# The last output tile of an attention and gated-FFN kernel in column blocks of 256, 128, 64 and 64

## The chip, the cores and the metric

The kernel runs on one core of a Trainium2 chip. In the profiles PE is TensorE, which does the matmuls, ACT is ScalarE, DVE is VectorE and SP is SyncE; a trailing q marks the engine's instruction queue, which waits and issues transfers while the engine itself counts as idle. L385 is line 385 of that run's kernel. The metric is the device time of one execution in microseconds. The profile gives one execution as a trace; its span runs from the first to the last instruction and is some 1.8 us shorter than the time.

One quantity of this document: the **tail**, from the start of the first matmul of the last output tile to the end of the span, read from a trace. "At 2.45 us" means 2.45 us after that first matmul. A store "lands" when the profile shows it finished. Positions in the tail, landings and ends are read from the packed traces in nanoseconds and rounded to 0.01 us, so a difference of two rounded times can be off by 0.01. The expectations were written from spans rounded to 0.1 us and so differ by up to 0.04: tails of 5.75 for 5.78, 6.00 and 5.96 for 6.01 and 5.99, 6.48 for 6.44; 2.53, 2.38 and 2.86 for the 2.55, 2.40 and 2.82 from the last issue to the end.

## The reference, cut to what matters

```
x: 8 batches, 8 heads, 512 rows, 64      state: 8, 8, 32, 64
xread = softmax(x state^T / 8) state     sread = softmax(state x^T / 8) x
y   = concat(xread, sread) as rows of 512            # 8 * (512 + 32) = 4352 rows
out = (relu(y w_gate) * (y w_val)) w_out             # d_ff = 1536, fp32 out
```

The output is written in tiles of 128 rows by 512 columns. Each tile is a sum over 12 slices of d_ff, that is 12 matmuls with 128x128 weights.

## The kernel before: the parts that matter

Matmul results lie in one of eight PSUM banks; output tiles alternate between two of them, 6 and 7. A copy by ScalarE or VectorE takes a result to one of four staging buffers, and a store takes it from there to memory.

```python
opool = pool("opool", 4)                              # four staging buffers "o_sb"
given, turn = [], {"r": 0, "o": 1}

def bank(name, kind="r"):
    if given:
        n = given.pop(0)                              # a bank named by hand
    ...
    else:
        n = turn["r"] % 6 if kind == "r" else 6 + turn["o"] % 2
        turn[kind] += 1
    return psum.tile([128, 512], FP32, name=name, tag=f"b{n}")

def fin_x(b, tsub, eng="act"):                        # an ordinary output tile
    o_sb = opool.tile([128, d_model], FP32, name="o_sb", tag="o_sb")
    copy[eng](out=o_sb, in_=held["o", b, tsub])
    n = 2 if b == B - 2 or (b == B - 1 and tsub == 0) else 1
    for i in range(n):                                # stored whole or in two halves of rows
        rows = slice(128 // n * i, 128 // n * (i + 1))
        nc.sync.dma_start(out=out_rows(b, tsub)[rows], in_=o_sb[rows])

def out_last(b, tsub):                                # the last tile, in column blocks
    for lo, n, eng, q in ((0, 256, nc.scalar.copy, nc.scalar), (256, 128, nc.scalar.copy, nc.scalar),
                          (384, 128, nc.vector.tensor_copy, nc.sync)):
        cols = slice(lo, lo + n)
        ps = o_bank()[:, 0:n]                         # bank("o_ps", "o"): 6 and 7 in turn
        for jf in range(NF):
            nc.tensor.matmul(ps, hsb[b][:, jf, ...], wo_sb[:, jf, cols], ...)
        o_sb = opool.tile([128, d_model], FP32, name="o_sb", tag="o_sb")
        eng(out=o_sb[:, 0:n], in_=ps)
        q.dma_start(out=out_rows(b, tsub)[:, cols], in_=o_sb[:, 0:n])
```

The softmax here doesn't subtract the row's maximum and nothing guards it: scores larger than these inputs give would overflow.

Of the kernel before, what the change touches and what calls it, by code (L numbers as in the profile page):

```python
# [16 lines left out]
def kernel(  # L17
# [9 lines left out]
    nc = tc.nc  # L27

    B, H, S, D = x.shape
# [316 lines left out]
    def o_bank():  # L346
        return bank("o_ps", "o")
# [8 lines left out]
    def out_rows(b, tsub):  # L356
        return out[b * SP: b * SP + S].rearrange("(p q) m -> q p m", q=NC)[tsub]

    def fin_x(b, tsub, eng="act"):
        o_sb = opool.tile([128, d_model], FP32, name="o_sb", tag="o_sb")  # L360
        copy[eng](out=o_sb, in_=held["o", b, tsub])  # L361
        n = 2 if b == B - 2 or (b == B - 1 and tsub == 0) else 1
        for i in range(n):
            rows = slice(128 // n * i, 128 // n * (i + 1))
            nc.sync.dma_start(out=out_rows(b, tsub)[rows], in_=o_sb[rows])
# [9 lines left out]
    def out_last(b, tsub):  # L375

        for lo, n, eng, q in ((0, 256, nc.scalar.copy, nc.scalar), (256, 128, nc.scalar.copy, nc.scalar),
                              (384, 128, nc.vector.tensor_copy, nc.sync)):
            cols = slice(lo, lo + n)
            ps = o_bank()[:, 0:n]  # L380
            for jf in range(NF):
                nc.tensor.matmul(ps, hsb[b][:, jf, tsub * 128:(tsub + 1) * 128], wo_sb[:, jf, cols],  # L382
                                 start=(jf == 0), stop=(jf == NF - 1))
# [3 lines that stand above are left out]
# [5 lines left out]
    def out_piece(b, i):  # L392
        out_part(b, i)
        if i % 3 == 2:
            fin_x(b, i // 3)
# [37 lines left out]
    def spin(n, cols=512):  # L433
        for i in range(n):
# [6 lines left out]
             "sc": att_sc, "ex": att_exp, "nr": att_sum, "nx": att_scale, "aT2": att_T2, "ao2": att_out2, "aT": att_T, "ao": att_out,  # L441
             "c": c_unit, "co": c_out, "u": u_unit, "uo": u_out, "gv": gv, "re": relu, "mu": mult, "o": out_part,
             "of": fin_x, "xn": x_next, "xp": x_pad, "sr": sr_mm, "sn": sr_norm}
    program = """
    dx.1.0.2 dx.1.1.2 stc.0.0.act stc.0.1.act xc.0.0.dve dw.0.0.128 spin.7 stT.0@4 xc.0.1.act dw.1.0.128 on xT.0.0@2
# [86 lines left out]
    for g in range(first, NF * (B + 1)):  # L532
        b, jf = divmod(g, NF)
# [14 lines left out]
    for i in range(NF - lag % NF, NF - 3):  # L548
        out_piece(B - 1, i)
    out_last(B - 1, NC - 1)  # L550


# [28 lines left out]
```

## Time and profile before

| | before |
|---|---|
| median time (6 runs, 222.99 to 223.83) | 223.5 us |
| span of the profiled run | 221.7 us |
| PE busy | 97% of the span |
| first matmul of the last tile | 215.95 us |
| issue of the last store | 219.17 us, so at 3.23 us |
| from that issue to the end of the span | 2.55 us |
| tail | 5.78 us |

The lines that show the tail are quoted in the prediction. This is the view of waits for SyncE in the last microseconds of the kernel before (engine and line, what it waited for: us in total, times, longest):

```profile
SPq L386 <- DVE o_sb L385: 2.0, 1, 2.0
SPq L365 <- ACT o_sb L361: 1.7, 1, 1.7
SPq L576 <- DMA out_dram<-o_sb: 0.8, 2, 0.4
SPq L576 <- PEq L576: 0.7, 2, 0.5
```

Line 576 is the end of the program. Two of its waits for stores took 0.4 us each, the rest found their store already landed.

### The profile page before, as it was taken

The numbers are of one execution on the slowest core, as the hardware profiler recorded it, in microseconds if no ns is written. First come the engines' busy times: TensorE is split into PE (matmuls) and PEld (weight loads), VectorE is DVE, ScalarE is ACT, GpSimd is POOL, SyncE is SP. The second block draws the span as 40 slices with busy tenths as digits, with TensorE's granted clock in tenths as the row PEclk, the third lists the DMA queues.
The fourth block names the chain that finished last, engine by engine and source line by source line (L and its number), as shares of the span: only waits on it lengthen the run. The fifth ranks groups of instructions, "written<-read, shape, count | busy, mean of one in ns | idle before, by whom it ended". The sixth has DMA issues, their size and how long they took to land.

```text
span 221.7 us, 4851 instructions
## 1 busy us (share of the span) xinstructions
PE 216.0 (97%) x1959; PEld 106.3 (48%) x1959; DVE 130.5 (59%) x228; ACT 124.8 (56%) x238; POOL 49.4 (22%) x54
## 2 busy tenths in 40 slices
PE   7799999999999999999999999999999999999994
PEld 3454455444554444444444444445444445666544
DVE  2697898965786569664767378646874433222100
ACT  5489888565767555564466456645654444222222
POOL 8777826460004233015000700000000000000000
PEclk9999999999999999999999999999999999999999
DMA  6999999182065962771169114501311112222332
GB/s 156 174 195 197 203 237 276 43 154 86 4 146 188 146 233 79 156 240 51 50 146 278 53 47 101 104 34 50 95 50 47 49 47 50 50 47 55 89 95 95
DMA packets 37879, 25.48 MB, mean 115 GB/s; under 512 B 18944, under 2 KB 33280, under 8 KB 37856
## 3 DMA queue, kind: packets, MB, share of 16 engines
q1 hardware_dynamic: 24992, 16.85, 28.7%
q0 software_dynamic: 11968, 7.47, 21.7%
q10 hardware_dynamic: 896, 0.85, 1.4%
q8 instruction: 15, 0.25, 0.5%
q14 instruction: 8, 0.07, 0.1%
HBM read 18.35 MB, written 8.91 MB: 123 GB/s over the span
## 4 chain that ended last, share of the span: by engine, by line
PE 85%; DMA 12%; POOL 1%; issue 0%; DVE 0%; POOLq 0%; DVEq 0%
PE o_ps L353 39%; PE gv_ps L316 32%; DMA xb<-in_x_dram 9%; PE gv_ps L333 5%; PE up L291 4%; DMA wg_sb<-in_moe_w_gate_dram 4%; PE sr_ps L264 1%; PE sc_ps L200 1%; PE o_ps L382 1%; PE xT_ps L186 0%; POOL xb L415 0%; PE stT_ps L129 0%; PE aT_ps L235 0%; PE srT_ps L277 0%; PE upc L291 0%
## 5 line engine op out<-in xcount | busy, mean ns | idle before, releaser
L353 PE MATMUL o_ps<-wo_sb,h_sb 128*128 128x512 bf16 x372 | 94.8, 379 | 0.0
L316 PE MATMUL gv_ps<-ans,U 128*128 128x512 bf16 x384 | 94.4, 379 | 0.0
L344 DVE TENSOR_TENSOR h_sb<-gv_ps,g_sb 128x512 bf16<-128x512 f32 x96 | 65.0, 689 | 43.5 <-ACT g_sb L340 42.1
L340 ACT ACTIVATE g_sb<-gv_ps 128x512 bf16<-128x512 f32 (+1 forms) x108 | 62.9, 588 | 45.9 <-PE gv_ps L316 35.0
L316 PEld LDWEIGHTS <-U 128*128 128x128 bf16 x384 | 36.1, 98 | 40.7 <-issue 0.4
L353 PEld LDWEIGHTS <-h_sb 128*128 128x128 bf16 x372 | 35.3, 98 | 39.7 <-issue 1.6
L361 ACT COPY o_sb<-o_ps 128x512 f32<-128x512 f32 x31 | 18.3, 590 | 17.4 <-PE o_ps L353 17.4
L301 ACT CAST U<-up 128x512 bf16<-128x512 f32 x36 | 18.9, 593 | 12.1 <-PE up L291 12.0
L142 POOL CAST xb<-xf 128x1024 bf16<-128x1024 f32 x10 | 10.6, 1088 | 66.4 <-DMA xf<-in_x_dram 45.4
L301 DVE CAST U<-up 128x512 bf16<-128x512 f32 x36 | 22.7, 684 | 4.1 <-PE up L291 3.7
L256 POOL COPY xa<-xb 128x2048 bf16<-128x2048 bf16 (+1 forms) x9 | 15.5, 1748 | 0.3
L213 DVE TENSOR_REDUCE cs<-e_sn 128x16 f32<-128x512 bf16 x16 | 10.9, 683 | 7.3 <-ACT e_sn L207 7.3
L344 DVE TENSOR_TENSOR hs_sb<-gv_ps,g_sb 128x256 bf16<-128x256 f32 x12 | 5.1, 425 | 15.3 <-PE gv_ps L333 10.8
L207 ACT ACTIVATE e_sn<-sc_ps 128x512 bf16<-128x512 f32 x16 | 9.6, 600 | 7.4 <-PE sc_ps L200 7.4
L219 DVE TENSOR_TENSOR a_sn<-e_sn,rc 128x512 bf16<-128x512 bf16 x16 | 12.4, 778 | 0.4
L291 PEld LDWEIGHTS <-stT 64*32 64x32 bf16 x512 | 5.9, 90 | 9.5 <-issue 8.1
L311 ACT CAST U<-upc 128x512 bf16<-128x512 f32 (+1 forms) x21 | 10.1, 570 | 0.5 <-PE upc L291 0.4
L200 PEld LDWEIGHTS <-xT 128*128 128x128 bf16 x128 | 5.7, 98 | 4.1 <-DVE xT L177 0.8
L291 PE MATMUL up<-wg_sb,stT 64*32 64x512 bf16 x144 | 7.5, 382 | 0.0
L291 PE MATMUL up<-wv_sb,stT 64*32 64x512 bf16 x144 | 7.2, 380 | 0.0
L333 PE MATMUL gv_ps<-br,wg_sb 128*128 128x256 bf16 x48 | 7.2, 273 | 0.0
L333 PE MATMUL gv_ps<-br,wv_sb 128*128 128x256 bf16 x48 | 7.2, 273 | 0.0
(63 smaller groups left out, 121.5 us busy)
## 6 DMA issues: line engine op xcount, KB each, us to landing
out_dram<-o_sb SPq DMA_DIRECT2D x26, 256.0 KB, 2.4
xf<-in_x_dram SPq DMA_DIRECT2D x4, 1024.0 KB, 6.3
wo_sb<-in_moe_w_out_dram POOLq DMA_DIRECT2D x2, 768.0 KB, 14.5
wg_sb<-in_moe_w_gate_dram POOLq DMA_DIRECT2D x5, 256.0 KB, 8.6
wv_sb<-in_moe_w_val_dram POOLq DMA_DIRECT2D x5, 256.0 KB, 10.5
out_dram<-o_sb SPq DMA_DIRECT2D x10, 128.0 KB, 2.4
xf<-in_x_dram POOLq DMA_DIRECT2D x1, 1024.0 KB, 16.1
xb<-in_x_dram POOLq DMA_DIRECT2D x3, 256.0 KB, 6.8
```

The lines of the kernel that those rows point to most:

```text
L142: copy[eng](out=xb[b][:, :, hs].rearrange("p c h d -> p h c d"), in_=xf[b][:, hs])
L213: nc.vector.reduce_sum(out=cs, in_=e_v, axis=AX.X)
L219: {"dve": nc.vector, "pool": nc.gpsimd}[eng].tensor_tensor(out=by_pair(a_sn[b], jp).rearrange("p r (j n) -> p r j n", n=Ns), in0=e_v, in1= ...
L256: nc.gpsimd.tensor_copy(out=v[:, hs:hs + src.shape[1]], in_=src)
L291: nc.tensor.matmul(dst[parity][32 * j:32 * j + 32], stT[r:r + 64, b, j, 32 * parity:32 * parity + 32], wsb[r:r + 64, j, lo:lo + n], start= ...
L301: copy[eng](out=U[b][:, w, kc, lo:lo + 512], in_=held["u", b, w, lo][kc])
L316: nc.tensor.matmul(ps[w], U[b][:, w, kc, f0:f0 + 128], ANS[b][:, kc].rearrange("p c t -> p (c t)"), start=(kc == 0), stop=(kc == NK - 1))
L333: nc.tensor.matmul(ps[w][:, 0:nt], wsb[:, j, f0:f0 + 128], br[:, j].rearrange("p b n -> p (b n)"), start=(j == 0), stop=(j == NJ - 1))
L340: nc.scalar.activation(out=g_sb[:, 0:n], in_=ps[0][:, 0:n], func=AF.Relu)
L344: nc.vector.tensor_tensor(out=dst, in0=ps[1][:, 0:n], in1=held["g", b, jf][:, 0:n], op=ALU.mult)
L353: nc.tensor.matmul(held["o", b, tsub], src[:, jf, tsub * 128:(tsub + 1) * 128], wo_sb[:, jf], start=(jf == 0), stop=(jf == NF - 1))
L361: copy[eng](out=o_sb, in_=held["o", b, tsub])
```

## The change

Its intent: the path after the last matmul is a copy, a store and the close. A last block of 64 columns in place of 128 makes that copy and that store smaller, while the rest of the columns are copied and stored beside the matmuls. One other store, 12 us ahead, becomes one transfer in place of two halves.

```diff
-        n = 2 if b == B - 2 or (b == B - 1 and tsub == 0) else 1
+        n = 2 if b == B - 2 else 1
...
-                              (384, 128, nc.vector.tensor_copy, nc.sync)):
+                              (384, 64, nc.vector.tensor_copy, nc.sync), (448, 64, nc.vector.tensor_copy, nc.sync)):
```

## The prediction

> **What bounds the kernel now.** I read the page first: PE is busy 97% of the span, so until about 218.8 us of a span of 221.7 us the matmuls set the time. The diff touches only the last tile, so I went to the end of the span. The chain of waits there (start us, us, what):
>
> ```profile
> by line: PE o_ps L353 55.9%; PE o_ps L382 15.7%; PE gv_ps L333 9.6%; DVE o_sb L385 1.7%; issue 0.3%; DVEq L385 0.2%
> ...
> 207.48 8.63 PE o_ps L353 x40
> 216.11 2.67 PE o_ps L382 x36
> 218.78 0.04 DVEq L385
> 218.81 0.04 issue
> 218.85 0.29 DVE o_sb L385
> ```
>
> The reader is to see that the 36 matmuls of the last tile (line 382: three blocks of 12) run without a gap behind the tile before, and that after them only one VectorE copy remains, then its store. The timeline shows who does what in that tail:
>
> ```profile
> 215.95 2.81 PE L382 MATMUL o_ps<-wo_sb,h_sb 128*128 128x256 bf16 x36
> 216.15 0.59 ACT L361 COPY o_sb<-o_ps 128x512 f32<-128x512 f32 x1 [2.00 <-PE o_ps L353]
> 216.76 0.35 SPq L365 DMA_DIRECT2D out_dram<-o_sb  x1
> 217.46 0.37 ACT L385 COPY o_sb<-o_ps 128x256 f32<-128x256 f32 x1 [0.72 <-PE o_ps L382]
> 217.86 0.36 ACTq L386 DMA_DIRECT2D out_dram<-o_sb  x1
> 218.39 0.27 ACT L385 COPY o_sb<-o_ps 128x128 f32<-128x128 f32 x1 [0.56 <-PE o_ps L382]
> 218.69 0.36 ACTq L386 DMA_DIRECT2D out_dram<-o_sb  x1
> 218.85 0.29 DVE L385 COPY o_sb<-o_ps 128x128 f32<-128x128 f32 x1 [10.84 <-PE o_ps L382]
> 219.17 0.35 SPq L386 DMA_DIRECT2D out_dram<-o_sb  x1
> ```
>
> Matmuls end at 215.95 + 2.81 = 218.76; VectorE starts 0.09 later, copies until 219.14; the store is issued at 219.17. The DMA view gives that store 1.6 us to landing, so 220.8; closing semaphores fill the last 0.9 us. After 218.76 only this one path matters: copy, issue, landing, close, 2.9 us in all. The change means to shorten the copy and the store on it.
>
> The 36 matmuls also fix the blocks in time. A burst of matmuls of 128 columns and one of 64 columns, both with 128x128 weights, stand elsewhere in the timeline:
>
> ```profile
> 45.56 0.39 PE L235 MATMUL aT_ps<-id,a_sn 128*128 128x128 bf16 x4
> 57.25 0.40 PE L200 MATMUL sc_ps<-stT,xT 128*128 128x64 bf16 x8
> ```
>
> One of 128 columns lasts 0.219 us and one of 64 lasts 0.193 us (groups by form). So the pitch is (0.39 - 0.219)/3 = 0.057 us at 128 columns and (0.40 - 0.193)/7 = 0.030 us at 64: half the columns cost half the time, and the weight load doesn't hold a 64-column stream. Counted back from 218.76, the last matmul starts at 218.54, the third block at 218.54 - 11 x 0.056 = 217.93, and the second ends at about 218.09.
>
> **What the Trainium skill says.** "TensorE: Matmul & The Clock Gate", section "Back-to-back issue gap", gives about 60 cycles (25 ns) for up to 64 columns and 134 for 128. The trace agrees within 5 ns (30 and 57 ns). "PSUM — Partial Sum Buffer", section "PSUM bank collisions raise a hardware error", says that a matmul writing and another engine reading the same bank must be kept apart by a semaphore, by bank and not by address. The trace before shows no PE wait in the tail, but this decides the case after the change. "VectorE: DVE Perf Modes", in the errata section, gives a PSUM read 120 cycles plus one per fp32 element: 258 ns at 128 elements, where the trace has 292; the page's fixed part is too small here, its slope fits. "DMA: Bandwidth & Descriptors", section "Specifications", says that runs under 512 B are read-modify-written; no store in the tail before has such runs (a row of 128 fp32 is just 512 B), so the trace can't confirm it for stores.
>
> **The change part by part.**
>
> First part: the store of tile 0 of the last batch becomes one DMA of 256 KB instead of two halves, near 203.8 us. It saves SyncE one issue of about 0.47 us (median of that line), while SyncE has nothing to do until about 209. Its buffer is taken again only at 216.15, some 12 us later. Worth 0.
>
> Second part: the last 128 columns become 64 + 64.
> - Matmuls: 12 x 0.056 = 0.67 us become 24 x 0.030 = 0.71 us: +0.04 if nothing waits.
> - Copy: the cast of 512 fp32 from PSUM takes 684 ns on VectorE and the copy of 128 takes 292, a slope of (684 - 292)/384 = 1.02 ns per element. At 64: 292 - 65 = 227 ns, so -0.065 on the path. The copy of the third block lies beside the matmuls of the fourth.
> - Store: 64 columns are 32 KB instead of 64, but still 128 rows. The store's data moves in about 0.4 us of its 1.6; I give it 0 to -0.1 from the smaller rows, with the read-modify-write as the opposite risk.
> - SyncE: with no wait the third block's copy would end near 218.77 and its issue run from 218.80 to 219.15, so the fourth's issue would start at 219.15: no gain against 219.17.
>
> So even undisturbed this is worth 0 to 0.1 us.
>
> **The new wait.** The output banks are two and alternate. Before, the tile before used one, block 1 the other, block 2 the first again, block 3 the one of block 1, freed at 217.46 + 0.37 = 217.83, just ahead of its use at 217.93. The fourth block needs the bank of block 2, which ScalarE reads from 218.39 to 218.66. (It starts that late, though the matmuls ended at 218.09, since ScalarE was issuing block 1's store until 218.22.) The third block's matmuls now start their last at 217.93 + 11 x 0.030 = 218.26; the fourth could start at 218.29, but must wait until 218.66 plus a semaphore. The wait of the first score matmuls for VectorE shows about 0.06 us from the end of the copy (5.54 + 0.82 = 6.36) to the matmul (6.42). So: first matmul 218.72; last 218.72 + 11 x 0.030 = 219.05; its end + 0.193 = 219.24; VectorE + 0.09 = 219.33; + 0.227 = 219.56; issue + 0.03 = 219.59. Against 219.17 that is **+0.42 us**. If the weight load is also held, add up to 0.1; for the smaller store take off up to 0.1. Sum: +0.4 us, 223.5 + 0.4 = 223.9 us.
>
> **The rivals.**
> - No bank wait in effect (ScalarE would read block 2 sooner, or the wait be shorter): 223.4 to 223.5. Against it: ScalarE's work before that copy isn't changed, so 218.66 should stand.
> - The staging buffers become the wait. There are four, and the fourth block takes the one of tile 2, whose store is issued at 216.76. At 2.0 us to landing (DMA view of the tail) it is free at 218.8, half a microsecond before the copy at 219.33. Hidden; if it landed 1 us late, it would add 0.5: 224.4.
> - The 256-byte rows cost more to write: if the store takes twice its data time, +0.4: 224.3. The trace has only reads of that size.
> - ScalarE or SyncE becomes the bound: SyncE's two issues are 0.35 each and, with the bank wait, 0.8 apart, so no.
>
> **Range and chances.** All of these move tenths of a microsecond. Three runs before spread from 222.99 to 223.83, so the noise is as large as the effect. From 223.2 (no wait, a low draw) to 224.5 (wait plus slow small rows). A change over 2% would need 4.5 us, more than the whole tail of 2.9 us after the last matmul. So within 2% is 0.98 likely; of the rest slower takes a little more.
>
> **What would show it.** In the changed trace: the pitch of line 382 near 0.030 us in the 64-column blocks; a gap of about 0.4 us in its matmuls, ended by ScalarE's copy of block 2; VectorE copies near 227 ns; the last SyncE issue about 0.4 us later; the single store of tile 0 without effect. I'd be wrong if the matmuls ran on without a gap, if the last copy waited for a DMA, or if the last store's landing differed clearly from 1.6 us.

## The result, and the profile after

The changed kernel takes 223.84 us median (six runs, 223.24 to 224.29) against 223.5; the ratio is 1.0016 with an interval of 0.9995 to 1.0037. Within 2%, as forecast, and 0.06 us from the forecast time.

The timeline of the tail of the changed kernel (start us, us, engine, line, what; in brackets the idle time ahead of it and what ended it):

```profile
216.50 2.49 PE L382 MATMUL o_ps<-wo_sb,h_sb 128*128 128x256 bf16 x36
218.42 0.36 ACTq L386 DMA_DIRECT2D out_dram<-o_sb  x1
218.95 0.27 ACT L385 COPY o_sb<-o_ps 128x128 f32<-128x128 f32 x1 [0.56 <-PE o_ps L382]
219.09 0.22 DVE L385 COPY o_sb<-o_ps 128x64 f32<-128x64 f32 x1 [10.52 <-PE o_ps L382]
219.26 0.51 PE L382 MATMUL o_ps<-wo_sb,h_sb 128*128 128x64 bf16 x12 [0.27 <-ACT o_sb L385]
219.34 1.11 SPq L386 DMA_DIRECT2D out_dram<-o_sb  x2
219.87 0.22 DVE L385 COPY o_sb<-o_ps 128x64 f32<-128x64 f32 x1 [0.55 <-PE o_ps L382]
```

The matmuls no longer run through. The first three blocks end at 216.50 + 2.49 = 218.99; then PE stands idle for 0.27 us until 219.26, and what ended that is ScalarE's copy, which ends at 218.95 + 0.27 = 219.22. The chain of what ended last says the same, step by step (start us, us, what):

```profile
218.01 0.38 ACT o_sb L385
218.40 0.02 issue
218.42 0.36 ACTq L386
...
218.95 0.28 ACT o_sb L385
219.22 0.04 issue
219.26 0.53 PE o_ps L382 x12
219.79 0.03 DVEq L385
219.82 0.04 issue
219.87 0.22 DVE o_sb L385
```

Before, this chain went straight down PE. Now it runs over ScalarE: copy of block 1, issue of block 1's store, copy of block 2, and only then the fourth block's matmuls.

The last store is issued at 220.12, which is 3.61 us after the first matmul at 216.50: 0.39 later than before. But the span ends only 6.01 us after that matmul, a tail 0.23 us longer. So 0.15 us came back after the last issue: 2.40 us from there to the end against 2.55.

### The profile page after: what moved, and what is told of

Read it like the earlier page. It is cut to its first block, busy times and chain, and to the rows that moved or that the text cites. A ratio compares the mean times of both kernels' runs of the same rounds, so it can differ in the third digit from the quotient of the medians.

```text
span 222.5 us, 4849 instructions
## 1 busy us (share of the span) xinstructions
PE 213.6 (96%) x1942; PEld 106.6 (48%) x1971; DVE 130.5 (59%) x229; ACT 124.7 (56%) x238; POOL 48.9 (22%) x54
## 4 chain that ended last, share of the span: by engine, by line
PE 93%; DMA 3%; issue 2%; ACT 0%; POOL 0%; ACTq 0%; DVE 0%; POOLq 0%; DVEq 0%
PE o_ps L353 38%; PE gv_ps L316 37%; PE gv_ps L333 5%; PE up L291 4%; DMA xb<-in_x_dram 3%; PE sc_ps L200 2%; PE upc L291 2%; PE sr_ps L264 1%; PE xT_ps L186 1%; PE o_ps L382 1%; PE warm_ps L435 1%; PE aT_ps L235 1%; PE xT_ps L173 0%; PE stT_ps L129 0%; ACT o_sb L385 0%
## 5 line engine op out<-in xcount | busy, mean ns | idle before, releaser
L316 PE MATMUL gv_ps<-ans,U 128*128 128x512 bf16 x372 | 93.1, 379 | 0.6 <-issue 0.2
L353 PE MATMUL o_ps<-wo_sb,h_sb 128*128 128x512 bf16 x358 | 91.8, 379 | 2.0 <-issue 1.7
L142 POOL CAST xb<-xf 128x1024 bf16<-128x1024 f32 x10 | 10.1, 1040 | 66.8 <-DMA xf<-in_x_dram 61.9
```

Of the source, the lines that this page charges most:

```text
L316: nc.tensor.matmul(ps[w], U[b][:, w, kc, f0:f0 + 128], ANS[b][:, kc].rearrange("p c t -> p (c t)"), start=(kc == 0), stop=(kc == NK - 1))
L353: nc.tensor.matmul(held["o", b, tsub], src[:, jf, tsub * 128:(tsub + 1) * 128], wo_sb[:, jf], start=(jf == 0), stop=(jf == NF - 1))
```

## The experiments

All tails in one table. "Lands after" is counted from the last store's issue. "Waits behind" counts SyncE's closing waits for other transfers that still follow the last store's own. "Close" is the time from the last store's issue to the end of the span. Ratios are to the kernel before, from five rounds; the changed kernel's is from the six runs of each.

| run | last store issued at | lands after | waits behind | close | tail | ratio (95%) |
|---|---|---|---|---|---|---|
| before | 3.23 | 1.63 | 0 | 2.55 | 5.78 | |
| changed | 3.61 | 1.47 | 0 | 2.40 | 6.01 | 1.0016 (0.9995 to 1.0037) |
| after_again | 3.62 | 1.47 | 0 | 2.38 | 5.99 | 1.0027 (1.0006 to 1.0048) |
| four_banks | 3.28 | 1.55 | 0 | 2.47 | 5.75 | 1.0013 (0.9993 to 1.0034) |
| store0_sync | 3.35 | 1.46 | 0 | 2.38 | 5.73 | 1.0017 (0.9999 to 1.0036) |
| three_blocks | 3.16 | 1.69 | 0 | 2.62 | 5.77 | 1.0001 (0.9983 to 1.0020) |
| store_only | 3.22 | 1.62 | 1 | 2.61 | 5.84 | |
| split_only | 3.62 | 1.47 | 7 | 2.82 | 6.44 | |
| same_bank | 3.72 | 1.47 | 0 | 2.39 | 6.11 | |
| last_128 | 3.95 | 1.61 | 0 | 2.54 | 6.48 | |
| four_banks_stage | 3.28 | 1.54 | 0 | 2.47 | 5.75 | 0.9986 (0.9965 to 1.0008) |
| free_store0_sync | 3.26 | 1.53 | 0 | 2.44 | 5.70 | 1.0003 (0.9971 to 1.0034) |
| one_more_store | 3.23 | 1.63 | 7 | 2.96 | 6.19 | 1.0002 (0.9972 to 1.0031) |
| merge_elsewhere | 3.62 | 1.46 | 0 | 2.39 | 6.01 | 0.9978 (0.9952 to 1.0003) |

The close is the landing plus a remainder. Where no wait stands behind the last store's, the remainder is 0.91 to 0.93 us in all eleven profiles.

How to weigh the two kinds of number: all the tails differ by at most 0.8 us, while the first matmul of the last tile started anywhere from 215.25 to 216.71 us in these profiles, with the same program in front of it but for single stores. That scatter of the 215 us ahead lies on every time and is larger than the effect, so the times can't rank these kernels. Part of it is the granted TensorE clock: every timed run whose mean clock was 0.991 or 0.992 took 223.77 us or more (median 224.27), while the median of the others was 223.28. In the profiles of that kind (the changed kernel's is one) the clock is 0.91 in the first 20 us, where the kernel before has 1.00. Steps inside the tail repeat to 0.01 us (3.61 and 3.62; ScalarE's store of block 2 at 2.74 in nearly all), so they can. Each tail is that of a single profile; three profiles with the changed kernel's last tile and as many stores (changed, after_again, merge_elsewhere) agree within 0.02.

### The changed kernel again

No edit; the control of that chip.

> The changed kernel once more, as the control of this chip. My theory (the fourth block waits for the output bank that ScalarE still reads): the matmuls of the last tile show a gap of about 0.3 to 0.4 us, ended by ScalarE; from the first matmul of the last tile to the start of the last store's issue 3.62 us, against 3.22 us in the kernel before; time 0.2 to 0.4 us over the kernel before. Rival (the two runs of times differ by chance): the time is within 0.1 us of the kernel before, and the 3.62 us don't come back.

Measured: gap of 0.27 us ended by ScalarE, last issue at 3.62, tail 5.99; time 223.6 against 223.1 median, ratio 1.0027. The gap and the late issue are properties of the kernel, not chance. This is also the one timed comparison whose interval lies above 1, by a little; two of its six runs had the lower clock and none of the eleven runs of the kernel before, so even this isn't a clean sign of the tail.

### A bank of its own for the fourth block

```diff
+            if lo == 448:
+                given.append(0)            # bank 0, idle since the gate and value matmuls
             ps = o_bank()[:, 0:n]
```

> The changed kernel with the fourth block in a bank of its own that nobody has used for 10 us. Bank theory: no gap in the matmuls of the last tile, from its first matmul to the last store's issue about 3.20 us (0.42 less than in the changed kernel), time equal to the kernel before or 0.1 us under it. Rival, the staging buffer: its store lands only about 0.1 us before the copy would now start, so if that wait takes over the copy starts up to 0.2 us later, 3.2 to 3.4 us. Rival, small rows or the extra issue cost the time: nothing is gained, time stays 0.3 us over the kernel before.

Measured: the matmuls run through, the last issue is back from 3.61 to 3.28, the tail from 6.01 to 5.75. The line of the 48 matmuls in this kernel's timeline, without a gap:

```profile
216.09 2.84 PE L384 MATMUL o_ps<-wo_sb,h_sb 128*128 128x256 bf16 x48
```

The bank wait is thus shown to be the cause of the later issue. The time, ratio 1.0013, doesn't resolve it. And the rival named for it came out: with the bank out of the way, the fourth copy waited for a staging buffer. Chain of what ended last, this kernel:

```profile
216.90 2.02 DMA out_dram<-o_sb
218.93 0.04 DVEq L387
...
219.10 0.23 DVE o_sb L387
```

The store of the tile before, issued at 216.90, holds one of the four buffers for 2.02 us; the fourth block is the fourth user after it and gets that very buffer. Its copy starts at 219.10 - 216.09 = 3.01 us.

### The fourth block in the bank of the third

```diff
+            if lo == 448:
+                given.append(6 + (turn["o"] + 1) % 2)     # the bank just used
             ps = o_bank()[:, 0:n]
```

> The changed kernel with the fourth block put into the bank of the third, the one that VectorE reads. Bank theory: the gap stays but is ended by VectorE's copy of the third block (ends about 2.81 us after the last tile's first matmul, ScalarE's ended at 2.71), so the fourth block starts at about 2.86 us in place of 2.76, the last store is issued at about 3.72 us and the tail is about 6.08 us. Rival (the gap comes from ScalarE or the weight loads, not from the bank): gap and releaser as in the changed kernel, 3.62 us.

Measured: issue at 3.72 and tail 6.11, as computed (6.08) within 0.03. The releaser changed with the bank (timeline of this kernel):

```profile
218.50 0.23 DVE L387 COPY o_sb<-o_ps 128x64 f32<-128x64 f32 x1 [10.52 <-PE o_ps L384]
...
218.78 0.51 PE L384 MATMUL o_ps<-wo_sb,h_sb 128*128 128x64 bf16 x12 [0.37 <-DVE o_sb L387]
```

The same matmuls now wait 0.37 us for VectorE, where they waited 0.27 for ScalarE. Whoever reads the bank decides: it is the bank, neither ScalarE as such nor the weight loads.

### The first block's store on SyncE

```diff
-        for lo, n, eng, q in ((0, 256, nc.scalar.copy, nc.scalar), ...
+        for lo, n, eng, q in ((0, 256, nc.scalar.copy, nc.sync), ...
```

> The changed kernel with the store of the first block issued by SyncE in place of ScalarE. Theory: ScalarE reads the second block late only because it is issuing a store, so its copy starts about 0.26 us sooner relative to the last tile's first matmul (2.18 in place of 2.45 us), the bank comes free as much sooner, and the last store's issue starts at about 3.38 us in place of 3.62. Rival: the copy waits for something else (the matmuls end later than I think), then it still starts at 2.45 and the tail stays 3.62 us.

Measured: ScalarE's copy of block 2 starts at 218.43 - 216.25 = 2.18 us in place of 2.45, exactly as forecast, and the fourth block follows it; last issue 3.35, tail 5.73. The lines in the timeline of this kernel:

```profile
218.43 0.27 ACT L385 COPY o_sb<-o_ps 128x128 f32<-128x128 f32 x1 [0.30 <-PE o_ps L382]
218.73 0.36 ACTq L386 DMA_DIRECT2D out_dram<-o_sb  x1
218.84 0.23 DVE L385 COPY o_sb<-o_ps 128x64 f32<-128x64 f32 x1 [10.52 <-PE o_ps L382]
219.35 0.22 DVE L385 COPY o_sb<-o_ps 128x64 f32<-128x64 f32 x1 [0.29 <-PE o_ps L382]
```

So ScalarE read block 2 late because its own queue was busy issuing a store. An issue counts as no busy time, and the profile puts that idle time down to PE; only the order of the lines, and the chain of the changed kernel above, show it.

### Three blocks: 256, 192 and 64

The kernel before, with these block widths.

```diff
-(256, 128, nc.scalar.copy, nc.scalar), (384, 128, nc.vector.tensor_copy, nc.sync)
+(256, 192, nc.scalar.copy, nc.scalar), (448, 64, nc.vector.tensor_copy, nc.sync)
```

> The kernel before with blocks of 256, 192 and 64 columns: the last copy and store are as short as in the changed kernel, but there is no fourth block and so no bank to wait for. Bank theory: no gap, last copy near 224 ns, last store's issue about 3.15 us after the last tile's first matmul (3.22 before), landing 1.5 us as in the changed kernel, time 0.1 to 0.2 us under the kernel before. Rival, rows of 256 bytes cost time: the store lands later than 1.6 us after its issue and the time isn't under the kernel before.

Measured: no gap, last issue at 3.16 as forecast, but the tail is 5.77, just that of the kernel before, and the ratio 1.0001. The 0.07 us won by the shorter copy was given back: the 32 KB store took 1.69 us to land. It follows ScalarE's 96 KB store by 0.31 us. The expectation of 1.5 us failed: a miss, and what its rival forecast for rows of 256 bytes. But the same rows landed in 1.47 us in the changed kernel, so the rows alone don't explain it.

### What the size of the last store is worth

Blocks of 256, 64, 64 and 128, so that a 64 KB store goes out last and far behind the others.

```diff
-(256, 128, ...scalar), (384, 64, ...vector), (448, 64, ...vector)
+(256, 64, ...scalar), (320, 64, ...vector), (384, 128, ...vector)
```

> Blocks of 256, 64, 64 and 128: the last store is again of 64 KB in rows of 512 bytes, but goes out over 1 us after the other stores. It measures what the size of the last store is worth by itself: the 64 KB store of the kernel before took 1.6 us with another issued 0.48 us ahead; the 32 KB one took 1.5 with 0.78 us of distance, 1.6 with 0.44 and 1.7 with 0.31. If the distance decides, this store takes 1.5 us; if the size decides, 1.6 us. The bank theory: fourth block starts when ScalarE has read the 64 columns of the second, at about 2.7 us, last store's issue at about 3.96 us.

Measured: issue at 3.95 as computed, 1.61 us to landing and a close of 2.54 us, though SyncE's store before it was issued 3.95 - 2.79 = 1.16 us ahead. The 64 KB store thus costs the same alone as 0.48 us behind another (1.63 and 2.55). The 32 KB store in rows of 256 bytes, 0.78 us behind, takes 1.47 and closes in 2.40 and 2.38. So half the size is worth about 0.15 us. The small store lands later the closer it follows another: 1.46 us at 0.51 behind, 1.53 to 1.55 at 0.42 to 0.44, 1.69 at 0.31. That nearness is the cause isn't shown: at 0.31 us the store ahead was also larger (96 KB, where the nearest was 32 KB in the others).

### Each part of the change alone

The first part alone, then the second alone:

```diff
-        n = 2 if b == B - 2 or (b == B - 1 and tsub == 0) else 1     # store_only: this line of the diff only
+        n = 2 if b == B - 2 else 1
```

> The first part of the change alone: the store of tile 0 of the last batch as one DMA. Theory: nothing on the path; from the first matmul of the last tile to the end of the span 5.75 us as in the kernel before (6.00 and 5.96 in the two profiles of the changed kernel). Rival (the longer single store holds a staging buffer or the queue): the tail grows toward 6.0 us.

Measured: issue at 3.22, tail 5.84. Nothing moved up to the landing, as expected; the 0.06 us more is one closing wait behind the last store's own, on which more below.

> The second part alone: the last 128 columns as 64 and 64, the store of tile 0 in two halves as before. Theory: the whole effect, 0.27 us gap in the matmuls ended by ScalarE, last store's issue at 3.62 us after the last tile's first matmul, tail 5.96 to 6.00 us. Rival (both parts needed): a tail nearer 5.75 us.

Measured: gap 0.27 us and issue at 3.62 as expected, but a tail of **6.44** us, 0.43 us more than the whole change, with the last store landing in the same 1.47 us. This fits no theory held until then. SyncE's waits at the end of the program (line 576), first in the changed kernel, then in the split alone:

```profile
SPq L576 <- PEq L576: 0.7, 2, 0.5
SPq L576 <- DMA out_dram<-o_sb: 0.5, 2, 0.4
```

```profile
SPq L576 <- DMA out_dram<-o_sb: 1.1, 1, 1.1
SPq L576 <- PEq L576: 0.7, 2, 0.5
```

In the changed kernel SyncE waits for stores twice, 0.4 us at most; in the split alone once, for 1.1 us. Looking at line 576 on SyncE only for 0.2 us (changed kernel) and 0.5 us (split alone) around and after the landing of the last store (operation, count, ns shortest/median/longest, first and last start), first the changed kernel, then the split alone:

```profile
L576 SPq EVENT_SEMAPHORE  x1: 28/28/28, 221.6 to 221.6; - x1
L576 SPq DRAIN  x1: 13/13/13, 221.7 to 221.7; - x1
```

```profile
L576 SPq EVENT_SEMAPHORE  x8: 27/28/28, 221.4 to 221.9; - x8
```

SyncE passes a list of waits one after the other, each for a semaphore, the counter by which a transfer reports that it has landed. In the changed kernel the last store's wait is the last of the list, and the others are worked off while that store is still under way. In the split alone it is the second of nine: SyncE blocks on it and then still has seven waits ahead, some 0.06 us apart, 0.43 us in all.

### Is it the number of stores?

The kernel before with one more store, and the change with another store merged in place of tile 0's:

```diff
-        n = 2 if b == B - 2 or (b == B - 1 and tsub == 0) else 1           # one_more_store, on the kernel before
+        n = 2 if b == B - 2 or (b == B - 1 and tsub < 2) else 1
-        n = 2 if b == B - 2 else 1                                         # merge_elsewhere, on the changed kernel
+        n = 2 if (b == B - 2 and tsub < 3) or (b == B - 1 and tsub == 0) else 1
```

> The kernel before with the store of tile 1 of the last batch in two halves as well: one store more, 8 us ahead of the last tile, and nothing else. The profile of the split alone ended 2.86 us after its last store's issue where the changed kernel took 2.38, with the same landing of 1.5 us; there SyncE passed eight more closing waits, 0.05 us each, after the last store had landed, in the changed kernel none. Count theory: the waits come in a fixed order and the stores take their semaphores in turn, so one store more puts the last store's wait first and about 0.45 us of waits behind it: here too the span ends about 3.0 us after the last issue (2.53 before), tail 6.2 us against 5.75, time about 0.4 us over the kernel before. Rival (the outlier came from the split, or from chance): 2.5 us and 5.75 us as before.

Measured: a tail of 6.19 us and a close of 2.96, with not one instruction of the last tile changed and the same 1.63 us to landing. The waits, first in the kernel before, then in this one, from the landing on, are one and eight with the last store's own, so seven behind it where the expectation had counted eight:

```profile
L576 SPq EVENT_SEMAPHORE  x1: 28/28/28, 220.8 to 220.8; - x1
```

```profile
L576 SPq EVENT_SEMAPHORE  x8: 27/28/28, 220.1 to 220.5; - x8
```

The time did not follow (ratio 1.0002, 0.9972 to 1.0031): 0.4 us is 0.0018 of the time, inside that interval.

> The split of the last tile, tile 0 of the last batch in two halves as before, but another store, tile 3 of the batch before it, made one in place of two: as many stores as in the changed kernel. Count theory: the end comes 2.35 to 2.40 us after the last issue and the tail is 5.96 to 6.00 us, as in the changed kernel and not 6.48 as in the split alone. Rival (that store of tile 0 itself matters): about 2.86 us and 6.4 us or more.

Measured: tail 6.01, close 2.39, as in the changed kernel. It is therefore the number of stores, which settles where in the closing list the last store's wait falls, and not that particular store. The packed traces bear it out by the semaphores' numbers. These transfers take eight semaphores in turn (100, 102, 103, 114 to 118, then 100 again), and SyncE's closing list has them in that order in every run. The last store has 118, the last of the list, in every run with as many stores as the kernel before; 117 with one store fewer (store_only), so one wait behind it; and 100, the first of the eight, with one more (split_only and one_more_store), so seven. Why the list is built that way was not looked into. The time, ratio 0.9978, was if anything under the kernel before, which the tail contradicts; such is the noise.

### Both waits removed

```diff
+            if lo == 448:
+                o_sb = gpool.tile([128, 512], BF16, name="g_sb", tag="g_sb").bitcast(FP32)   # idle for 10 us
+            else:
                 o_sb = opool.tile([128, d_model], FP32, name="o_sb", tag="o_sb")
```

This goes on top of the fourth block's own bank. A fifth staging buffer, the simpler way, did not fit: the build asked for 10 KB per partition and had 8.7 left.

> As the kernel with a bank of its own for the fourth block, and its copy goes to a staging buffer that nobody has used for 10 us. In that kernel the chain showed the copy waiting for a store of the tile before (2.02 us to landing), copy start 3.01 us after the last tile's first matmul. Theory: with both waits gone the copy starts at 2.95 us, ended by the matmuls, and the last store is issued at 3.2 us, as SyncE is then busy with the third block's store until 3.19; tail 5.65 to 5.70 us against 5.75 before. Time within 0.1 us of the kernel before, which these runs cannot resolve. Rival: some further wait, copy still at 3.0 us or later.

Measured: the copy starts at 218.49 - 215.60 = 2.89 us, 0.12 earlier than with the staging wait and released by the matmuls. Yet the last issue is at 3.28 as before: the copy ends at 3.11, but SyncE is still issuing the third block's store, from 2.84 for 0.35 us, and begins the next only 0.09 us after that. The forecast of 5.65 to 5.70 for the tail failed: it is 5.75 with a close of 2.47, both as with the staging wait. That wait had delayed the copy, but nothing behind it: SyncE's issue of the third block's store came next.

With the first block's store on SyncE besides:

```diff
-        for lo, n, eng, q in ((0, 256, nc.scalar.copy, nc.scalar), ...
+        for lo, n, eng, q in ((0, 256, nc.scalar.copy, nc.sync), ...
```

> The last kernel with the first block's store on SyncE besides, so that ScalarE reads the second block 0.26 us sooner and its store is further from the last one. Theory: last store's issue again at 3.2 us, now 0.7 us behind ScalarE's store (0.44 before), landing 1.5 to 1.6 us, tail 5.60 to 5.65 us, the shortest of all; time 0.1 to 0.15 us under the kernel before. Rival: the third block's store, issued just ahead on the same queue, sets the landing, and the tail is 5.7 us as without the move.

Measured: last issue at 3.26, landing 1.53, tail 5.70 us, the shortest of all, 0.08 us under the kernel before but above the 5.60 to 5.65 expected; ratio 1.0003. No version is shown to beat the kernel before: the best of the fourteen tails is worth under 0.04% of the time.

## Why the prediction was right, point by point

- **The bound and the order of size.** Right. Only the tail changed, and it changed by tenths of a microsecond. The forecast of 223.9 us met 223.84, but with a scatter of about 1 us between runs that nearness is luck; what was right is the mechanism.
- **The bank wait.** Right in kind and size: a gap ended by ScalarE's copy of block 2, last issue 0.39 us later against +0.42 computed. The sign "a gap of about 0.4 us" mixed two counts: by the prediction's own times the fourth block starts 218.72 - 218.29 = 0.43 us late, but the idle time that a trace shows begins at the end of the matmul before: 218.72 - 218.26 - 0.193 = 0.27, and 0.27 was measured. Giving the block a bank of its own, and changing who reads its bank, showed the cause.
- **ScalarE late because it issues a store.** Right; moving that issue moved the copy by 0.27 us.
- **Matmul pitch and copy.** Right: the waiting block of 12 took 0.51 us against 11 x 0.030 + 0.193 = 0.52; the copy 224 ns against 227.
- **The store's term, "0 to -0.1".** Too small: the close shrank by 0.15 us (2.55 to 2.40), all of it in the landing. So the tail grew by 0.23 us, where the sum said 0.4. The rival, that 256-byte rows add 0.4 us, fell: these stores landed in 1.47 us, sooner than the 1.63 of the wide ones. A smaller cost of such rows isn't excluded, since they came with half the bytes.
- **"Worth 0" for the first part.** This step was wrong, though no number of the sum suffered: alone that part costs 0.06 us, one closing wait, but beside the split it holds the number of stores where it was, and without it the close is 0.42 us longer (2.82 against 2.40). The cost of a store was counted as its issue and its buffer; its place among the closing waits was missed. The issue of "about 0.47 us (median of that line)" was misread, too: the median of the line is 0.34, and the two halves took 0.47 and 0.60 where the single store took 0.34. Nothing waited for it.
- **Staging buffers hidden.** Right for the changed kernel; with the bank wait gone they held the copy up by 0.12 us, but not the last issue.
- **"Even undisturbed 0 to 0.1 us", with SyncE's issues as the limit.** Right: without the bank wait the tail was 5.75, with neither wait 5.75, against 5.78. With both waits gone the last issue came at 3.28, behind the third block's, where the prediction had put it at 219.15, that is at 3.20.

## What to carry to other kernels

Before a tail is cut into more pieces, count the buffers that each piece takes in turn: with two banks and four staging buffers a fourth block waits for the second block's reader and, next, for the store of the tile before, and the matmuls that should hide everything stand still. Behind these stood SyncE's issue of the third block's store, so lifting the waits gained 0.03 us in all over the kernel before. What is issued last should have its closing wait last; adding one store, 8 us ahead, moved the end by 0.41 us here. And where the effect is smaller than the scatter of the whole, compare steps from a fixed point close to the change, not times.

## What the Trainium skill lacked or had wrong

- No page has that the waits at the end of a program are passed one by one in a fixed order, some 0.06 us each, so that the number of stores decides whether up to seven of them follow the last landing: close 2.96 us with one store more, 2.55 without.
- "DMA: Bandwidth & Descriptors", section "Specifications", warns of runs under 512 B. Here a 32 KB store in rows of 256 bytes landed in 1.47 us, a 64 KB one in rows of 512 bytes in 1.63, so no large penalty showed (1.69 us, 0.31 us behind a 96 KB store, was the latest). No run has 32 KB in rows of 512 bytes, so a penalty smaller than what half the bytes save would not show.
- "VectorE: DVE Perf Modes", in the errata section: 120 cycles plus one per element gives (120 + 64)/0.96 = 192 ns for the copy of 64 fp32 from PSUM; measured 224. The slope of about 1 ns per element held (292 ns at 128).
- "Trainium Kernel Development and Optimization", section "Key Constraints", says that issuing stores from several engines saves only the issue time. In a tail that is not little: ScalarE's issue of 0.36 us delayed its next copy by 0.27 us, and PE after it.
